# A six-operation exponential on VectorE and a shorter run-up to the first exponential, in a fused attention and feed-forward kernel

## The chip, the cores and the metric

One core of a Trainium2 chip runs the program. The metric is device time in microseconds (us), lower is better. Most executions of one kernel here lie within some 2.5 us of their median, so a difference below a few tenths of a per cent needs several rounds; the ratios below come with a 95% interval. The times go with the TensorE clock that was granted: the kernel before spanned 881.2 us in the run with a mean clock of 0.999 and 885.7 us in one with 0.993.

Engine names in the profile: PE is TensorE (PEld its weight loads), ACT is ScalarE, DVE is VectorE, POOL is GpSimd, SP issues most transfers.

## The reference

```python
def reference(A_x, A_wqkv, A_wo, B_x, B_w_gate, B_w_up, B_w_down, gate_w):   # S=2048, D=512, 32 heads of 16, F=1792
    x = A_x
    g = sigmoid((x * gate_w).sum(-1, keepdims=True))
    a = attention(x, wqkv, wo)        # softmax(q k^T / 4) v, per head, then wo
    b = (silu(x @ w_gate) * (x @ w_up)) @ w_down
    return g * a + (1 - g) * b
```

What matters is the softmax: 32 heads x 2048 queries x 2048 keys, 134 million exponentials. The kernel cuts them into 2048 score tiles of 128 keys x 512 queries.

## The kernel before

TensorE makes a score tile in PSUM. Two tiles at a time go to ScalarE, which does the exponential in one activation of 128x1024 (`e_t<-s_t`). Every so often four tiles go to VectorE instead: each is scaled and rounded to a 16-bit integer whose upper bits are those of a bf16 exponent (`y_t<-d_t`), and a polynomial in the low nine bits then corrects the mantissa over all four tiles at once.

```python
def first():        # once per tile; after the fourth tile, queue the passes over [128, 2048]
    vec.tensor_scalar(out=y[:, i*QBW:(i+1)*QBW], in0=d_t, scalar1=EXP_A, scalar2=EXP_B, op0=mult, op1=add)
    ...
    vops.extend([                    # (cost in us that the kernel's own plan charges VectorE, the pass)
        (0.73, z = y & 0x1FF),
        (0.73, u = C3*z + C2),
        (1.26, u = u * z),
        (0.73, u = (u + C1) * S),
        (1.26, u = u * z),
        (1.26, y = y + u),
        (0.73, y = y * 0.25; the block may now be multiplied with the values)])
```

That listing is abridged: each entry is a lambda around one VectorE instruction. While the program is built, a planner keeps three clocks (`plan.pe`, `plan.act`, `plan.dve`) and decides from them when VectorE is free enough to take another block. So the charged cost of a block decides how many blocks VectorE gets, and with them the order of every engine.

The run-up to the first exponential, abridged:

```python
def v_now(tt): ...                       # four matmuls of value tile tt, evacuated by ScalarE
act(out=q0r, in_=qp0, func=Copy)
for i in range(2):                       # two halves of the keys of the first heads
    vec.tensor_reduce(out=kpart0[:, i], in_=kp0[i], op=max, apply_absolute_value=True)
    vec.tensor_copy(out=ones_h[i], in_=onescol)
    v_now(i)
    act(out=kaug[...i...], in_=kp0[i], func=Identity, bias=ones_h[i])
    if i == 0: kneg1 = bsel0 * kpart0[:, 0];  aq0 = |q0r|
kneg0 = min(bsel0 * kpart0[:, 1], kneg1)
v_now(2)
mm(bp0, lhsT=kneg0, rhs=aq0)             # a bound on the scores, kept below zero in the exponent
...                                      # q0 <- q0r, then q0 += bp0
V0 = 4
v_now(3)                                 # the first exponential follows; values from V0 on are paced side work
```

Later query blocks get the same bound by `q0_pieces(qb)`: it evacuates the projection, writes |q| to `mt[:, 4:6, :]`, and a separate piece, `bound`, multiplies it. The paced side work (values, keys, queries, the feed-forward part) is placed between score tiles by deadline.

Of the kernel before, what the change touches and what calls it, by code (L numbers as in the profile page):

```python
# [9 lines left out]
ALU = mybir.AluOpType  # L10
# [68 lines left out]
def kernel(  # L79
# [12 lines left out]
    nc = tc.nc  # L92
# [4 lines left out]
    DH = 16  # L97
# [19 lines left out]



    EXP_A = 512.0 * inv_sqrt_dh * math.log2(math.e)  # L120
    EXP_B = 512.0 * 127.0

    EXP_C3, EXP_C2, EXP_C1, EXP_S = 0.0012034477878222, 1.8215637461803453, -1248.848130748923, 1.0 / 4096.0



# [32 lines left out]
    def act(*args, **kw):  # L159
        ordered(nc.scalar.activation(*args, **kw))  # L160
# [7 lines left out]
    vec = Ordered()  # L168
# [49 lines left out]
    bsel0 = mt[:, 3, 0:P]  # L218
# [3 lines left out]
    for i in range(2):  # L222
        nc.vector.tensor_copy(
            out=wpad[i][:, :, :].rearrange("p dc (j c) -> p dc j c", c=32)[:, :, :, 1:1 + DH],
# [9 lines left out]
    pidx = const.tile([P, 1], F32, name="pidx")  # L234
    nc.gpsimd.iota(pidx[:], pattern=[[0, 1]], base=0, channel_multiplier=1,
                   allow_small_or_imprecise_dtypes=True)
    bsel = const.tile([P, 8], BF16, name="bsel")
    lo_t = const.tile([P, 8], F32, name="lo_t")
    for h in range(8):
        c = 2 * (h % 4) + h // 4  # L240
        nc.gpsimd.memset(lo_t[:, c:c + 1], float(DH * h))
    far_t = const.tile([P, 8], F32, name="far_t")

    nc.vector.tensor_scalar(out=lo_t[:], in0=lo_t[:], scalar1=pidx[:, 0:1], scalar2=None, op0=ALU.subtract)
    nc.vector.tensor_scalar(out=far_t[:], in0=lo_t[:], scalar1=-float(DH) + 0.5, scalar2=-1.0,
                            op0=ALU.is_gt, op1=ALU.mult)
    nc.vector.scalar_tensor_tensor(out=bsel[:, :], in0=lo_t[:], scalar=0.5, in1=far_t[:],
                                   op0=ALU.is_lt, op1=ALU.mult)
    nc.gpsimd.memset(wo_l[:], 0.0)
    sbc_t = const.tile([P, P], BF16, name="sbc_t")  # L250
    nc.gpsimd.memset(sbc_t[:], 0.0)
# [31 lines left out]
    def spend(mode, mms, ready=0.0):  # L283

        plan.pe = max(plan.pe + (0.1 if mode != plan.mode else 0.0), ready) + (0.226 if mode == "F" else 0.216) * mms
        plan.mode = mode
# [93 lines left out]
    def v_pieces(tt, act_evac=False):  # L380
        st = {}

        def pc(h):
            def f():
                if h == 0:
                    st["p"] = m_tile("vp")
                for dc in (2 * h, 2 * h + 1):
                    mm(st["p"][:, 0:D], lhsT=xT[:, dc, tt * P:(tt + 1) * P], rhs=wv[:, dc, :],
                       start=(dc == 0), stop=(dc == DC - 1))
                spend("F", 2)  # L390
                if h == 1 and act_evac:
                    end()
                elif h == 1:
                    later(0.75, end)
            return f

        def end():
            dst = vaug[:, tt, 0:G * 4 * VC].rearrange("p (h c) -> p h c", c=VC)[:, :, 1:1 + DH]
            sv = st["p"][:, 0:D].rearrange("p (h c) -> p h c", c=DH)
            if act_evac:  # L400
                act(out=dst, in_=sv, func=ACT.Copy)
            else:
                vec.tensor_copy(out=dst, in_=sv)
            m_free(plan.pe if act_evac else plan.dve)
        return [(2, pc(0), True), (2, pc(1), False)]
# [201 lines left out]
    def score(ps, b):  # L607
        n, j = b // 4, HEADS[b % 4]
        (qb, g), kt = UNIT[n // KT], n % KT
        r = slice(64 * (j // 2), 64 * (j // 2) + 64)  # L610
        q = q0[qb][r, j % 2, :] if g == 0 else get_qx(qb, g // 2)[r, j % 2, g % 2, :]
        mm(ps, lhsT=kaug[r, g, kt * P:(kt + 1) * P], rhs=q, start=True, stop=True,
           tile_position=(64 * (j // 2), 0))
# [26 lines left out]
    def emit_d(b):  # L640
        while d_wait:
            pay_d()
        d_t = ps_d.tile([P, QBW], F32, tag="d", name="d_t")
        score(d_t[:, :], b)
        spend("R", 1, d_end[0])
        if not vcur:
            y_live[0] += 1
            blocks[b // (4 * KT)] = blocks.get(b // (4 * KT), 0) + 1
            vcur["y"] = vex.tile([P, NV * QBW], U16, tag="y", name="y_t", bufs=3)
            vcur["i"], vcur["b"] = 0, []  # L650
        y, i = vcur["y"], vcur["i"]
        vcur["i"] += 1
        vcur["b"].append(b)
        e_of[b] = y[:, i * QBW:(i + 1) * QBW].bitcast(BF16)
        block = dict(vcur)
        if i == NV - 1:
            vcur.clear()

        def first():
            vec.tensor_scalar(out=y[:, i * QBW:(i + 1) * QBW], in0=d_t[:, :], scalar1=EXP_A, scalar2=EXP_B,  # L660
                              op0=ALU.mult, op1=ALU.add)
            if i < NV - 1:
                return
            z = vex.tile([P, NV * QBW], U16, tag="z", name="z_t")
            u = vex.tile([P, NV * QBW], F16, tag="u", name="u_t")
            ya, za, ua = y[:, :], z[:, :], u[:, :]
            mine = list(block["b"])
            assert sorted(m % 4 for m in mine) == list(range(4)) and mine[0] // (4 * KT) == mine[-1] // (4 * KT)
            vops.extend([
                (0.73, lambda: vec.tensor_scalar(out=za, in0=ya, scalar1=0x1FF, scalar2=None, op0=ALU.bitwise_and)),  # L670
                (0.73, lambda: vec.tensor_scalar(out=ua, in0=za, scalar1=EXP_C3, scalar2=EXP_C2, op0=ALU.mult,
                                                 op1=ALU.add)),
                (1.26, lambda: vec.tensor_tensor(out=ua, in0=ua, in1=za, op=ALU.mult)),
                (0.73, lambda: vec.tensor_scalar(out=ua, in0=ua, scalar1=EXP_C1, scalar2=EXP_S, op0=ALU.add,
                                                 op1=ALU.mult)),
                (1.26, lambda: vec.tensor_tensor(out=ua, in0=ua, in1=za, op=ALU.mult)),
                (1.26, lambda: vec.tensor_tensor(out=ya, in0=ya, in1=ua, op=ALU.add)),
                (0.73, lambda: (vec.tensor_scalar(out=ya, in0=ya, scalar1=0.25, scalar2=None, op0=ALU.mult),
                                late.append((plan.dve + 0.4, mine)))),
            ])  # L680
        d_wait.append((plan.pe + 0.25, first))

    def pay_d():
        ready, f = d_wait.pop()
        plan.dve = max(plan.dve, ready) + 0.6
        f()
        d_end[0] = plan.dve + 0.1
# [178 lines left out]
    kpart0 = const.tile([P, 2], F32, name="kpart0")  # L866
# [4 lines left out]
    kneg1 = mt[:, 3, 2 * P:3 * P]  # L871
    def v_now(tt):
        for _, f, _ in v_pieces(tt, act_evac=True):
            f()

    act(out=q0r[:, :], in_=qp0[:, :], func=ACT.Copy)
    for i in range(2):
        vec.tensor_reduce(out=kpart0[:, i:i + 1], in_=kp0[i][:, :], axis=AX.X, op=ALU.max,
                          apply_absolute_value=True)
        vec.tensor_copy(out=ones_h[i][:], in_=onescol[:])  # L880
        v_now(i)
        act(out=kaug[:, 0, i * 2 * QBW:(i + 1) * 2 * QBW], in_=kp0[i][:, :], func=ACT.Identity,
            bias=ones_h[i][:, 0:1], scale=1.0)
        if i == 0:
            vec.tensor_scalar(out=kneg1, in0=bsel0, scalar1=kpart0[:, 0:1], scalar2=None, op0=ALU.mult)
            vec.tensor_scalar(out=aq0[:, :].bitcast(U16), in0=q0r[:, :].bitcast(U16), scalar1=0x7FFF, scalar2=None,
                              op0=ALU.bitwise_and)
    vec.scalar_tensor_tensor(out=kneg0, in0=bsel0, scalar=kpart0[:, 1:2], in1=kneg1,
                             op0=ALU.mult, op1=ALU.min)
    v_now(2)  # L890
    bp0 = ps_d.tile([P, QBW], F32, tag="d", name="bp0")
    mm(bp0[:, :], lhsT=kneg0, rhs=aq0[:, :], start=True, stop=True)
    for v in range(2):
# [1 line left out]
    for v in range(2):  # L895
        vec.scalar_tensor_tensor(out=q0[0][:, v, :], in0=bp0[:, :], scalar=vsel[:, v:v + 1],
                                 in1=q0[0][:, v, :], op0=ALU.mult, op1=ALU.add)
    V0 = 4
    v_now(3)
    plan.dve = plan.act = plan.pe  # L900


# [2 lines left out]
    v_chain = {}  # L905
    for tt in range(V0, KT):
        v_chain[tt] = pace.add(v_pieces(tt), 0, tt + 3)
# [37 lines left out]
    for qb in range(QB):  # L945
        a0 = f0 + per * qb
        for fc in range(FC):
            load, pcs = gu[(qb, fc)]
            i = order_.index((qb, fc))
# [269 lines left out]
```

## Time and profile before

| | before |
|---|---|
| median of 3 runs | 885.43 us (884.97 to 886.7) |
| span of the profiled run | 883.3 us |
| exponentials on ScalarE / blocks on VectorE | 890 / 67 |
| first exponential starts | 19.82 us |
| end of the last exponential to the end | 8.8 us |

How to read the lines: a group line gives the source line (here mostly a helper's), the engine, the operation, output<-input, shapes and count; then busy time and mean nanoseconds of one; then the engine's idle time ahead of it and what ended that idle time. The prediction below shows the lines of the kernel before.

I use one more measure. ScalarE runs the exponentials almost back to back, and its step from one start to the next has a floor of 903 ns after an exponential and 477 ns after a tanh. What a step has above its floor I call a **slip**. Slips are summed from the start times in the trace, from the first exponential to the last: 24.1 us before. (The prediction and some expectations count only slips after exponentials, above 903.5 or 905 ns; that is 0.3 to 0.8 us less.)

Not every slip need be the program's. In each of the fourteen profiles TensorE's clock stood at half in one to three stretches of about 3.4 or 6.8 us between the first exponential and the last. The view of busy time by stretch shows it, here for such a stretch before, then after (columns: stretch, its length, busy time and number of instructions of PE, PEld, DVE, ACT, POOL, then the clock, and share and GB/s of the transfers):

```profile
859.69:866.51 6.82, 5.62 (x26) 1.27 (x26) 4.08 (x8) 5.38 (x7) 0.00 (x0) 0.50 0.01 2
```

```profile
842.83:846.24 3.41, 3.17 (x23) 0.73 (x19) 3.21 (x6) 2.84 (x4) 0.00 (x0) 0.50 0.01 2
```

The slips whose step ends in such a stretch, or within 1 us of its end, come to 1.9 us before and 1.0 after, and to 1.2 to 6.0 in the other profiles. Why the clock falls is not shown here. Below, "outside half clock" means slips without these.

### The profile page before, as it was taken

The page shows a single profiled execution, that of the slowest core. Times are in us where ns is not written, and L with a number is a line of the kernel's source. Part 1 is how long each engine was busy: PE and PEld are TensorE (multiplying, and loading weights), DVE is VectorE, ACT ScalarE, POOL GpSimd, SP SyncE. Part 2 cuts the span into 40 slices and gives each one's busy share as a digit, 9 for nine tenths or more (in the row PEclk, how much of TensorE's full clock was granted, in tenths as well). Part 3 has the DMA queues.
Part 4 walks back from the last instruction along what each step waited for, and adds up shares of the span by engine and source line. Part 5 has one row for each costly group of instructions (what it writes and reads, how often), then busy time and mean ns, then how long its engine had stood idle before and what let it go on. Part 6 is the DMA issues. An engine that isn't in the chain of part 4 may idle for free.

```text
span 883.3 us, 14242 instructions
## 1 busy us (share of the span) xinstructions
PE 784.8 (89%) x5078; PEld 207.2 (23%) x5168; DVE 797.8 (90%) x1129; ACT 853.5 (97%) x955; POOL 7.0 (1%) x29
## 2 busy tenths in 40 slices
PE   6999999999998898889998888998988888989876
PEld 2222222222222222222222222222222222222211
DVE  6379999999999999998999999999999999999995
ACT  3999999999999999999999999999999999999995
POOL 3000000000000000000000000000000000000000
PEclk9999999999999999999999999999999999999998
DMA  8401021121101112110001112100011111000000
GB/s 208 108 1 33 23 50 43 34 49 28 34 7 31 34 43 64 45 34 16 5 11 35 38 42 61 48 24 10 4 32 34 36 51 44 22 11 5 4 21 24
DMA packets 87535, 31.98 MB, mean 36 GB/s; under 512 B 75120, under 2 KB 87016, under 8 KB 87464
## 3 DMA queue, kind: packets, MB, share of 16 engines
q1 hardware_dynamic: 86408, 30.94, 14.3%
q8 instruction: 40, 0.66, 0.3%
q10 hardware_dynamic: 1056, 0.13, 0.1%
q14 instruction: 31, 0.25, 0.1%
HBM read 20.83 MB, written 2.34 MB: 26 GB/s over the span
## 4 chain that ended last, share of the span: by engine, by line
ACT 40%; PE 29%; DVE 17%; issue 10%; SPq 1%; DMA 1%; DVEq 0%; ACTq 0%
ACT e_t L160 37%; PE s_t L157 11%; DVE y_t L166 7%; PE o_ps L157 6%; DVE u_t L166 5%; ACT th L160 3%; PE d_t L157 3%; PE dps L157 2%; PE gp L157 2%; PE qp L157 1%; PE up L157 1%; SPq L173 1%; DVE mt L166 1%; PE kp L157 1%; DVE gs L166 1%
## 5 line engine op out<-in xcount | busy, mean ns | idle before, releaser
L160 ACT ACTIVATE e_t<-s_t 128x1024 bf16<-128x1024 f32 x890 | 830.3, 1080 | 7.0 <-PE s_t L157 6.0
L157 PE MATMUL s_t<-qx,kaug 64*128 64x512 bf16 x1668 | 333.3, 385 | 59.9 <-ACT e_t L160 55.8
L166 DVE TENSOR_SCALAR y_t<-d_t 128x512 uint16<-128x512 f32 x268 | 184.0, 687 | 28.0 <-PE d_t L157 25.1
L157 PEld LDWEIGHTS <-kaug 64*128 64x128 bf16 x2048 | 99.3, 93 | 389.3 <-issue 387.6
L157 PE MATMUL o_ps<-e_t,vaug 128*32 128x512 bf16 x1780 | 173.1, 388 | 0.9
L166 DVE TENSOR_TENSOR u_t<-u_t,z_t 128x2048 f16<-128x2048 f16 x134 | 163.4, 1219 | 1.9
L157 PE MATMUL d_t<-qx,kaug 64*128 64x512 bf16 x252 | 95.0, 377 | 1.7 <-DVE y_t L166 1.3
L166 DVE TENSOR_TENSOR y_t<-y_t,u_t 128x2048 uint16<-128x2048 uint16 x67 | 81.6, 1218 | 0.8
L157 PEld LDWEIGHTS <-vaug 128*32 128x32 bf16 x2048 | 45.4, 94 | 136.8 <-issue 133.2
L157 PE MATMUL dps<-wd_t,mt 128*128 128x512 bf16 x200 | 62.4, 384 | 3.3 <-issue 3.3
L157 PE MATMUL gp<-xT,wg 128*128 128x512 bf16 x196 | 61.6, 384 | 2.5 <-issue 2.5
L157 PE MATMUL up<-xT,wu 128*128 128x512 bf16 x210 | 62.4, 383 | 1.5 <-issue 1.4
L166 DVE TENSOR_SCALAR y_t<-y_t 128x2048 uint16<-128x2048 uint16 x67 | 46.2, 690 | 1.3
L166 DVE TENSOR_SCALAR u_t<-z_t 128x2048 f16<-128x2048 uint16 x67 | 46.0, 686 | 0.6
L166 DVE TENSOR_SCALAR u_t<-u_t 128x2048 f16<-128x2048 f16 x67 | 45.8, 684 | 0.2
L166 DVE TENSOR_SCALAR z_t<-y_t 128x2048 uint16<-128x2048 uint16 x67 | 45.9, 685 | 0.1
L166 DVE SCALAR_TENSOR_TENSOR gs<-th,gp 128x512 bf16<-128x512 bf16 x56 | 38.2, 682 | 5.1 <-ACT th L160 4.4
L166 DVE SCALAR_TENSOR_TENSOR mt<-gs,up 128x512 bf16<-128x512 bf16 x56 | 38.2, 683 | 3.5 <-PE up L157 1.7
L160 ACT ACTIVATE th<-gp 128x512 bf16<-128x512 f32 x56 | 36.8, 657 | 0.0
L157 PEld LDWEIGHTS <-mt 128*128 128x128 bf16 x263 | 16.2, 99 | 43.8 <-issue 36.8
L157 PE MATMUL s_t<-on,kaug 64*128 64x512 bf16 x112 | 22.0, 384 | 3.3 <-ACT e_t L160 3.2
L166 DVE TENSOR_TENSOR osb<-of,x_ps 128x512 bf16<-128x512 f32 x28 | 19.1, 681 | 2.8 <-PE x_ps L157 2.7
(101 smaller groups left out, 337.8 us busy)
## 6 DMA issues: line engine op xcount, KB each, us to landing
wg<-in_B_w_gate_dram SPq DMA_DIRECT2D x56, 128.0 KB
wu<-in_B_w_up_dram SPq DMA_DIRECT2D x56, 128.0 KB
on<-osb SPq DMA_DIRECT2D x120, 16.0 KB
rb<-rr SPq DMA_DIRECT2D x15, 128.0 KB
wd_t<-in_B_w_down_dram SPq DMA_DIRECT2D x1, 1792.0 KB
qx<-qst SPq DMA_DIRECT2D x112, 16.0 KB
out_dram<-o_t SPq DMA_DIRECT2D x12, 128.0 KB
kaug<-on SPq DMA_DIRECT2D x20, 64.0 KB
```

The costliest lines, as they stand in the source:

```text
L157: ordered(nc.tensor.matmul(*args, **kw))
L160: ordered(nc.scalar.activation(*args, **kw))
L166: return lambda *a, **kw: ordered(f(*a, **kw))
L173: nc.sync.dma_start_transpose(out=xT[:, dc, :], in_=x[:, dc * P:(dc + 1) * P])
```

## The change

The intent is threefold. The cubic in z is factored, so that a pass disappears: with z' = z + 2048 (an OR), the correction is (K z' + M)^2 z' plus a constant D, which rides on the last pass. Only two value tiles are made ahead of the first exponential, and the key copies come ahead of the value evacuations on ScalarE. Three tiny constants are made after the first scores.

```diff
-    EXP_B = 512.0 * 127.0
-    EXP_C3, EXP_C2, EXP_C1, EXP_S = 0.0012034477878222, 1.8215637461803453, -1248.848130748923, 1.0 / 4096.0
+    EXP_K, EXP_M, EXP_D = 0.0005430666826427128, -1.2590564982977572, -43.5
+    EXP_B = 512.0 * 127.0 + (-44.13360029727899 - EXP_D)
 ... (vops)
-  z = y & 0x1FF;  u = C3*z + C2;  u = u*z;  u = (u + C1)*S;  u = u*z;  y = y + u;  y = y*0.25
+  z = y & 0x1FF | 0x800;  u = K*z + M;  u = u*u;  u = u*z;  y = y + u;  y = (y + D)*0.25
 ... (run-up)
         vec.tensor_copy(out=ones_h[i][:], in_=onescol[:])
-        v_now(i)
         act(out=kaug[...], in_=kp0[i][:, :], func=ACT.Identity, bias=ones_h[i][:, 0:1], scale=1.0)
         if i == 0:
-            vec.tensor_scalar(out=kneg1, in0=bsel0, scalar1=kpart0[:, 0:1], ...)
             vec.tensor_scalar(out=aq0, in0=q0r, scalar1=0x7FFF, op0=ALU.bitwise_and)
+        v_now(i)
+    vec.tensor_scalar(out=kneg1, in0=bsel0, scalar1=kpart0[:, 0:1], ...)
     vec.scalar_tensor_tensor(out=kneg0, ...)
-    v_now(2)
 ...
-    V0 = 4
-    v_now(3)
+    lo_t, far_t, bsel: three small VectorE instructions, formerly ahead of the first maximum
+    V0 = 2
```

More of the change, by code (lines that the diff above doesn't have):

```diff
@@ L242 @@
     far_t = const.tile([P, 8], F32, name="far_t")
-    nc.vector.tensor_scalar(out=lo_t[:], in0=lo_t[:], scalar1=pidx[:, 0:1], scalar2=None, op0=ALU.subtract)
-    nc.vector.tensor_scalar(out=far_t[:], in0=lo_t[:], scalar1=-float(DH) + 0.5, scalar2=-1.0,
-                            op0=ALU.is_gt, op1=ALU.mult)
-    nc.vector.scalar_tensor_tensor(out=bsel[:, :], in0=lo_t[:], scalar=0.5, in1=far_t[:],
-                                   op0=ALU.is_lt, op1=ALU.mult)
     nc.gpsimd.memset(wo_l[:], 0.0)
@@ L669, in first @@
             vops.extend([
-                (0.73, lambda: vec.tensor_scalar(out=za, in0=ya, scalar1=0x1FF, scalar2=None, op0=ALU.bitwise_and)),
-                (0.73, lambda: vec.tensor_scalar(out=ua, in0=za, scalar1=EXP_C3, scalar2=EXP_C2, op0=ALU.mult,
+                (0.73, lambda: vec.tensor_scalar(out=za, in0=ya, scalar1=0x1FF, scalar2=0x800, op0=ALU.bitwise_and,
+                                                 op1=ALU.bitwise_or)),
+                (0.73, lambda: vec.tensor_scalar(out=ua, in0=za, scalar1=EXP_K, scalar2=EXP_M, op0=ALU.mult,
                                                  op1=ALU.add)),
-                (1.26, lambda: vec.tensor_tensor(out=ua, in0=ua, in1=za, op=ALU.mult)),
-                (0.73, lambda: vec.tensor_scalar(out=ua, in0=ua, scalar1=EXP_C1, scalar2=EXP_S, op0=ALU.add,
-                                                 op1=ALU.mult)),
+                (1.26, lambda: vec.tensor_tensor(out=ua, in0=ua, in1=ua, op=ALU.mult)),
                 (1.26, lambda: vec.tensor_tensor(out=ua, in0=ua, in1=za, op=ALU.mult)),
                 (1.26, lambda: vec.tensor_tensor(out=ya, in0=ya, in1=ua, op=ALU.add)),
-                (0.73, lambda: (vec.tensor_scalar(out=ya, in0=ya, scalar1=0.25, scalar2=None, op0=ALU.mult),
+                (0.73, lambda: (vec.tensor_scalar(out=ya, in0=ya, scalar1=EXP_D, scalar2=0.25, op0=ALU.add,
+                                                  op1=ALU.mult),
                                 late.append((plan.dve + 0.4, mine)))),
@@ L884 @@
         if i == 0:
-            vec.tensor_scalar(out=kneg1, in0=bsel0, scalar1=kpart0[:, 0:1], scalar2=None, op0=ALU.mult)
             vec.tensor_scalar(out=aq0[:, :].bitcast(U16), in0=q0r[:, :].bitcast(U16), scalar1=0x7FFF, scalar2=None,
                               op0=ALU.bitwise_and)
+        v_now(i)
+    vec.tensor_scalar(out=kneg1, in0=bsel0, scalar1=kpart0[:, 0:1], scalar2=None, op0=ALU.mult)
     vec.scalar_tensor_tensor(out=kneg0, in0=bsel0, scalar=kpart0[:, 1:2], in1=kneg1,
                              op0=ALU.mult, op1=ALU.min)
-    v_now(2)
     bp0 = ps_d.tile([P, QBW], F32, tag="d", name="bp0")
@@ L897 @@
                                  in1=q0[0][:, v, :], op0=ALU.mult, op1=ALU.add)
-    V0 = 4
-    v_now(3)
+    vec.tensor_scalar(out=lo_t[:], in0=lo_t[:], scalar1=pidx[:, 0:1], scalar2=None, op0=ALU.subtract)
+    vec.tensor_scalar(out=far_t[:], in0=lo_t[:], scalar1=-float(DH) + 0.5, scalar2=-1.0,
+                            op0=ALU.is_gt, op1=ALU.mult)
+    vec.scalar_tensor_tensor(out=bsel[:, :], in0=lo_t[:], scalar=0.5, in1=far_t[:],
+                                   op0=ALU.is_lt, op1=ALU.mult)
+    V0 = 2
     plan.dve = plan.act = plan.pe
```

## The prediction

> **What bounds the kernel now.** I read the page from the top: first the busy line, then the chain that ended last, then the costliest groups.
>
> ```profile
> PE 784.8 (89%) x5078; PEld 207.2 (23%) x5168; DVE 797.8 (90%) x1129; ACT 853.5 (97%) x955; POOL 7.0 (1%) x29
> ...
> ACT 40%; PE 29%; DVE 17%; issue 10%; SPq 1%; DMA 1%; DVEq 0%; ACTq 0%
> ...
> L160 ACT ACTIVATE e_t<-s_t 128x1024 bf16<-128x1024 f32 x890 | 830.3, 1080 | 7.0 <-PE s_t L157 6.0
> ...
> L166 DVE TENSOR_SCALAR y_t<-d_t 128x512 uint16<-128x512 f32 x268 | 184.0, 687 | 28.0 <-PE d_t L157 25.1
> L166 DVE TENSOR_TENSOR u_t<-u_t,z_t 128x2048 f16<-128x2048 f16 x134 | 163.4, 1219 | 1.9
> L166 DVE TENSOR_TENSOR y_t<-y_t,u_t 128x2048 uint16<-128x2048 uint16 x67 | 81.6, 1218 | 0.8
> L166 DVE TENSOR_SCALAR y_t<-y_t 128x2048 uint16<-128x2048 uint16 x67 | 46.2, 690 | 1.3
> L166 DVE TENSOR_SCALAR u_t<-z_t 128x2048 f16<-128x2048 uint16 x67 | 46.0, 686 | 0.6
> L166 DVE TENSOR_SCALAR u_t<-u_t 128x2048 f16<-128x2048 f16 x67 | 45.8, 684 | 0.2
> L166 DVE TENSOR_SCALAR z_t<-y_t 128x2048 uint16<-128x2048 uint16 x67 | 45.9, 685 | 0.1
> ```
>
> The reader is to see three things. ScalarE (ACT) is busy 97% of an 883.3 us span, and the 890 exponentials of 128x1024 were held up for only 7.0 us that the groups show as idle. VectorE (DVE) and TensorE (PE) are each near 90%, so neither has much to spare. And 2048 score tiles of 128x512 are shared between two engines: 890 x 2 = 1780 go to ScalarE, 268 = 67 blocks of four go to VectorE, which spends the last seven operations on each block. The chain gives ScalarE only 40%, because it hops at each step between three nearly full engines; I trust the busy line here.
>
> ScalarE's cost of one exponential is not the 1080 ns of the group, since neighbours overlap. From the start times in the trace, 577 of the 890 start-to-start steps are below 910 ns, and their floor is 903 ns. A tanh takes 477 ns of ScalarE in the same measure. So the ScalarE line adds up: first exponential at 19.82, 890 x 0.9035 = 804.1, 56 x 0.477 = 26.7, about 23.3 of steps longer than the floor (TensorE late by 0.1 to 1.2 us some 60 times, and many slips of 20 ns), about 0.5 for the gate's tanh, and 8.7 from the end of the last exponential to the end of the program: 883.1 against a span of 883.3.
>
> Ahead of the first exponential ScalarE is not full, so I took the order of time of the first 20 us (start, duration, engine, what):
>
> ```profile
> 13.47 1.23 DVE L166 TENSOR_REDUCE kpart<-kp 128x1 f32<-128x1024 f32 x1 [0.99 <-PE kp L157]
> ...
> 15.19 1.22 DVE L166 TENSOR_REDUCE kpart<-kp 128x1 f32<-128x1024 f32 x1
> 15.91 0.60 ACT L160 ACTIVATE vaug<-vp 128x512 bf16<-128x512 f32 x1 [1.19 <-PE vp L157]
> ...
> 16.44 0.35 DVE L166 SCALAR_TENSOR_TENSOR mt<-mt,kpart 128x128 bf16<-128x128 bf16 x1
> ...
> 17.44 0.38 PE L157 MATMUL bp<-aq,mt 128*128 128x512 bf16 x1
> ...
> 17.85 1.41 DVE L166 SCALAR_TENSOR_TENSOR qx<-bp,vsel,qx 128x512 bf16<-128x512 f32 x2 [0.53 <-PE bp L157]
> ...
> 18.05 1.02 PE L157 MATMUL vp<-rb,xT 128*128 128x512 bf16 x4 [0.23 <-ACT vaug L160]
> ...
> 18.87 1.10 ACT L160 ACTIVATE vaug<-vp 128x512 bf16<-128x512 f32 x2
> 19.00 0.70 PE L157 MATMUL s_t<-qx,kaug 64*128 64x512 bf16 x4
> ```
>
> The bound's matmul (bp) had its operand at 16.44 + 0.35 = 16.79 but ran at 17.44, behind twelve value matmuls. The first pair of score matmuls needs only the first half of qx (ready about 17.85 + 0.70 = 18.55), yet ran at 19.00, behind the fourth value tile, and the exponential came at 19.82 behind that tile's evacuation on ScalarE. The two extra value tiles are what the start waits for.
>
> **What the Trainium skill says.** "VectorE: DVE Perf Modes", section "The perf-mode tier table", gives for 2048 bf16 elements in SBUF 693 ns for tensor_scalar and 1224 ns for tensor_tensor, and says that single-source operations reach twice the rate. The trace agrees: 684 to 690 and 1218 to 1219 ns, for uint16 and f16 as well. "DVE: scalar operands, raw-bit mode, write accounting and state across instructions", section "Raw-bit mode", has AND and OR exact on a zero-extended uint16 stream, so a fused AND, OR should be one pass; no row here shows the fused pair yet. "ScalarE: Activation LUTs", section "What ACT_TABLE_LOAD costs", has an activation with immediate scale and bias at 186 + 0.833 N ns with neighbours overlapping by about 93 ns: 186 + 853 - 93 = 946 ns for N = 1024. The trace has 903, and I use 903. "Perfetto Trace Analysis", section "Identifying the Most-Contended Engine", has the engine with the highest occupancy as the one to optimize first, and warns that TensorE's matmul busy share says little; that fits the choice of ScalarE.
>
> **The change, part by part.**
>
> (a) *One VectorE pass less per block.* The removed pass is the tensor_scalar u_t<-u_t of 684 ns. The square u*u is a tensor_tensor in place of u*z (both 1219, assuming that reading one tile twice costs as reading two); the OR and the final add ride as second operations in passes that exist. A block goes from 4 x 0.687 + 4 x 0.686 + 3 x 1.219 = 9.15 us (four evacuations of d_t, four passes, three products or sums) to 8.46 us. On VectorE by itself this is worth nothing to the end, as VectorE is not the bound.
>
> (b) *What it frees is turned into more blocks.* The kernel hands out tiles as it is built, so I built the changed kernel and counted its order of instructions, which holds no times. It has 71 blocks in place of 67: 882 exponentials of 128x1024, 284 evacuations of d_t. TensorE's matmuls are the same in number and shape. ScalarE therefore loses 8 x 0.9035 = **7.2 us**, all of it on the bounding line. VectorE's exponentials go from 67 x 9.15 = 613 to 71 x 8.46 = 601 us; two more value evacuations at 0.69 bring VectorE to about 797.8 - 12 + 1.4 = 787 us, still about 90% of a shorter span.
>
> (c) *The start.* Two value tiles (eight matmuls, two 0.5 us evacuations on ScalarE) leave. In the new order ScalarE takes the first key copy ahead of the first value evacuation, and TensorE has eight value matmuls, the bound, then the scores. My timing: first maximum 13.47 to 14.70 as now; the 128x1 copy and |q| (0.28) follow; second maximum at about 15.0 instead of 15.19; kneg is no earlier, as both its steps (0.25 and 0.35) now follow the second maximum: ready about 16.8. The value matmuls end about 16.7 (14.85 + 8 x 0.22), so bp runs near 16.95 to 17.35, the first half of qx is done by 18.1, scores run 18.15 to 18.55, and the first exponential starts near 18.7 rather than 19.82: **1.1 us**. ScalarE is free by then (last evacuation about 17.9). So both maxima in a row gain almost nothing, and the missing value tiles nearly all.
>
> (d) *The small constants* (0.11 + 0.16 + 0.16 us on VectorE) move behind qx, where VectorE idles 1.45 us. Worth under 0.1 us.
>
> (e) *Given back.* 1.75 us of value matmuls now fall among the first exponentials, where TensorE is fullest (18.64 us of matmul records in the stretch from 20 to 40). TensorE's total wait for ScalarE is 59.0 us in the view of waits; the same matmuls must fit in 8 us less, so the 23.3 us of slips may grow. I choose +0.9 us, a twenty-fifth of the slips.
>
> Sum: -7.2 - 1.1 + 0.9 = -7.4, from 885.43 to **878.0 us** (0.8% faster).
>
> **The rivals.** *TensorE becomes the bound.* For it: 89% busy, slips of ScalarE that all end on s_t, and more blocks mean more lone d_t and x_ps work. Against it: 59 us of waits for ScalarE, spread over 158 places. If half the saving were lost, the time would be about 881.5. *VectorE runs late.* The kernel's order assumes 0.73 and 1.26 us for passes (measured 0.69 and 1.22) but 0.6 for evacuations (0.69). A block of the new kind is 0.09 us dearer than assumed, of the old kind 0.05, so TensorE may meet y_t not yet written; those waits (o_ps and x_ps on y_t or gs) are 7.5 us now. Doubled, they would put the time at 882 to 885. *The fused passes fall out of the fast mode*: a tensor_scalar at the 1.2 us rate would add some 0.5 us x 71 per pass, 36 us on VectorE, and make it the bound, 890 or more. The existing two-operation passes at 684 ns speak against it. *Better than the sum*: VectorE has lower load and the slips shrink by 3 us, giving 874.
>
> **Range and chances.** The 7.2 is a count by a measured floor and nearly sure; the start is sure to some 0.4 us; the slips are the doubt, from -3 to +4 us. That makes 874.0 to 882.0 for eight in ten. Two per cent is 17.7 us, over twice all that I can add up: 0.02 for faster. Slower by two per cent needs a fallen perf mode: 0.02.
>
> **What would show it right or wrong.** In the changed profile: 882 e_t activations with the floor at 903 ns; three tensor_scalar passes and three tensor_tensor passes of 71 each at 0.69 and 1.22 us, no fourth; VectorE near 787 us; first exponential at 18.5 to 19.0; tail after the last exponential 8.7 us as now; ScalarE's slips near 24 us. It is wrong if e_t's idle goes well above 10 us with PE s_t as its releaser, if a fused pass takes over 0.8 us, or if the first exponential does not move.

## The result

The changed kernel took **878.49 us** (median of 4 runs, 877.44 to 881.16); the kernel before, with a run beside it, 885.59. The ratio is 0.9923, interval 0.9899 to 0.9947. Ratios in this document divide the mean time of one kernel's runs by that of the other's of the same rounds, so they are not quite the ratio of the quoted medians. Outputs were correct in all kernels shown here. In numbers the prediction of 878.0 was met. The experiments show that two of its terms were wrong and cancelled.

The page of the changed kernel, the busy line and the groups that answer to those shown of before:

```profile
PE 783.2 (89%) x5076; PEld 206.5 (24%) x5168; DVE 789.5 (90%) x1104; ACT 845.4 (97%) x945; POOL 7.0 (1%) x29
...
L161 ACT ACTIVATE e_t<-s_t 128x1024 bf16<-128x1024 f32 x882 | 823.4, 1084 | 7.6 <-PE s_t L158 5.8
...
L167 DVE TENSOR_SCALAR y_t<-d_t 128x512 uint16<-128x512 f32 x284 | 195.1, 687 | 29.1 <-PE d_t L158 25.4
...
L167 DVE TENSOR_TENSOR u_t<-u_t 128x2048 f16<-128x2048 f16 x71 | 86.6, 1220 | 1.0
L167 DVE TENSOR_TENSOR y_t<-y_t,u_t 128x2048 uint16<-128x2048 uint16 x71 | 86.6, 1219 | 1.0
L167 DVE TENSOR_TENSOR u_t<-u_t,z_t 128x2048 f16<-128x2048 f16 x71 | 86.3, 1215 | 0.3
...
L167 DVE TENSOR_SCALAR y_t<-y_t 128x2048 uint16<-128x2048 uint16 x71 | 48.8, 688 | 1.0
L167 DVE TENSOR_SCALAR u_t<-z_t 128x2048 f16<-128x2048 uint16 x71 | 48.8, 687 | 0.8
L167 DVE TENSOR_SCALAR z_t<-y_t 128x2048 uint16<-128x2048 uint16 x71 | 48.6, 684 | 0.1
```

The count of exponentials went from 890 to 882, and the removed pass is gone: six passes of 71. The fused AND, OR takes 684 ns, as the AND alone took 685; the square of one tile takes 1220 ns, as the product of two took 1219. ScalarE is as full as before (97%), VectorE too (90%): what the pass freed was spent on more blocks.

The two profiled runs add up as follows.

| us | before | after | difference |
|---|---|---|---|
| start of the first exponential | 19.8 | 19.6 | -0.2 |
| exponentials at the 903 ns floor | 803.7 (890) | 796.4 (882) | -7.2 |
| slips ahead of 150 us | 3.1 | 6.8 | +3.7 |
| slips after 150 us | 21.0 | 17.0 | -4.0 |
| last exponential's end to the end | 8.8 | 8.8 | 0.0 |
| sum of differences (56 tanh unchanged) | | | -7.7 |
| span | 883.3 | 875.7 | -7.6 |

Of the later slips, 1.9 us before and 1.0 after are those at half clock, so the fall outside half clock is from 19.1 to 16.0: 3.1 us, not 4.0. The tail of 8.8 us is not fixed either: in four of the later profiles, with the clock at half during it, it was 9.8 to 10.3 us.

The third row is new, and no stretch at half clock lies in it. It also shows in the view of busy time by stretch, without any sum of mine: the row from 20 to 150 us of each kernel, first before, then after (columns: stretch, its length, then busy time and number of instructions for PE, PEld, DVE, ACT, POOL, then clock and transfers).

```profile
20.00:150.00 130.00, 121.48 (x805) 33.49 (x817) 105.33 (x152) 129.42 (x145) 0.00 (x0) 1.00 0.18 44
```

```profile
20.00:150.00 130.00, 119.37 (x787) 32.53 (x801) 103.48 (x150) 126.06 (x140) 0.00 (x0) 1.00 0.18 42
```

ScalarE is busy 129.42 of 130 us before and 126.06 after, with five instructions fewer done by then. Something in the changed kernel leaves ScalarE waiting early on.

The start, in order of time, of the changed kernel:

```profile
6.09 1.97 DVE L224 COPY mt<-wqk 128x256 bf16<-128x256 bf16 x1 [1.76 <-DMA wqk<-in_A_wqkv_dram]
6.13 1.81 POOL L405 MEMSET qx<- 128x2048 bf16 x1
...
14.58 1.23 DVE L167 TENSOR_REDUCE kpart<-kp 128x1 f32<-128x1024 f32 x1 [1.82 <-PE kp L158]
...
15.71 1.89 PE L158 MATMUL vp<-rb,xT 128*128 128x512 bf16 x8 [0.52 <-DMA rb<-in_A_wqkv_dram]
...
15.90 1.11 ACT L161 ACTIVATE kaug<-kp,ones_h 128x1024 bf16<-128x1024 f32 x1
...
17.95 0.39 PE L158 MATMUL bp<-aq,mt 128*128 128x512 bf16 x1 [0.36 <-DVE mt L167]
...
19.18 0.39 PE L158 MATMUL s_t<-qx,kaug 64*128 64x512 bf16 x2 [0.84 <-DVE qx L167]
19.61 5.12 ACT L161 ACTIVATE e_t<-s_t 128x1024 bf16<-128x1024 f32 x5 [0.62 <-PE s_t L158]
```

From the first maximum to the first exponential it is now 19.61 - 14.58 = 5.03 us, against 19.82 - 13.47 = 6.35 before: 1.3 us shorter. But this run's first maximum was 1.1 us later. The first two lines show why: the weights landed a little late, the copy that pads them met the GpSimd fill of another buffer, and a copy of 0.26 us took 1.97.

### The profile page after: what moved, and what is told of

It is laid out like the page before. It is cut to its first block, busy times and chain, and to the rows that moved or that the text cites. A ratio compares the mean times of both kernels' runs of the same rounds, so it can differ in the third digit from the quotient of the medians. Undisturbed runs are those within 1.5% of the kernel's fastest.

```text
span 875.7 us, 14203 instructions
## 1 busy us (share of the span) xinstructions
PE 783.2 (89%) x5076; PEld 206.5 (24%) x5168; DVE 789.5 (90%) x1104; ACT 845.4 (97%) x945; POOL 7.0 (1%) x29
## 4 chain that ended last, share of the span: by engine, by line
ACT 40%; PE 38%; DVE 10%; issue 10%; DMA 1%; ACTq 0%; DVEq 0%; SPq 0%
ACT e_t L161 37%; PE s_t L158 14%; PE o_ps L158 7%; DVE y_t L167 4%; PE d_t L158 4%; PE dps L158 3%; ACT th L161 3%; PE gp L158 2%; DVE u_t L167 2%; PE up L158 2%; PE kp L158 2%; PE qp L158 1%; PE vp L158 1%; PE a_ps L158 1%; DVE mt L167 1%
## 5 line engine op out<-in xcount | busy, mean ns | idle before, releaser
L167 DVE TENSOR_SCALAR y_t<-d_t 128x512 uint16<-128x512 f32 x284 | 195.1, 687 | 29.1 <-PE d_t L158 25.4
L158 PE MATMUL d_t<-qx,kaug 64*128 64x512 bf16 x264 | 99.7, 377 | 0.3
L167 DVE TENSOR_TENSOR u_t<-u_t 128x2048 f16<-128x2048 f16 x71 | 86.6, 1220 | 1.0
L167 DVE TENSOR_TENSOR y_t<-y_t,u_t 128x2048 uint16<-128x2048 uint16 x71 | 86.6, 1219 | 1.0
L167 DVE TENSOR_TENSOR u_t<-u_t,z_t 128x2048 f16<-128x2048 f16 x71 | 86.3, 1215 | 0.3
L167 DVE TENSOR_SCALAR y_t<-y_t 128x2048 uint16<-128x2048 uint16 x71 | 48.8, 688 | 1.0
L167 DVE TENSOR_SCALAR u_t<-z_t 128x2048 f16<-128x2048 uint16 x71 | 48.8, 687 | 0.8
L167 DVE TENSOR_SCALAR z_t<-y_t 128x2048 uint16<-128x2048 uint16 x71 | 48.6, 684 | 0.1
L167 DVE CAST vaug<-vp 128x512 bf16<-128x512 f32 x14 | 9.7, 691 | 15.5 <-PE vp L158 15.5
```

The costliest lines, as they stand in the source:

```text
L158: ordered(nc.tensor.matmul(*args, **kw))
L167: return lambda *a, **kw: ordered(f(*a, **kw))
```

## The experiments

The theories. **A**: the number of exponentials on ScalarE sets the time; VectorE's relief pays only through it. **B**: VectorE's relief itself pays. **C**: slips eat a part of what the exponentials give. **D**: the shorter start pays what it saves. Against D, after the first results, **E**, **F** and **J**: the two deferred value tiles take the gain back early on, by one misplaced bound (E), by projections that land among VectorE's exponentials (J), or by crowding in general (F). **G**: the collision with GpSimd costs time. **H**: VectorE has no more room. Twelve kernels ran, each with five rounds beside the kernel before. Whatever follows from one profile each is said so.

### One pass fewer, the same hand-out

The plan still charges seven passes; one entry issues nothing. TensorE's and ScalarE's orders are identical to those of before.

```diff
-  u = C3*z + C2;  u = u*z;  u = (u + C1)*S  (0.73);  u = u*z; ...
+  u = K*z + M;    u = u*u;  nothing         (0.73);  u = u*z; ...      # and the new constants
```

> The six-operation exponential in the kernel before, while the hand-out of tiles still charges VectorE for the seventh pass (an entry that issues nothing). TensorE's and ScalarE's orders are then the same as before, 890 exponentials, 67 blocks; VectorE just has 67 x 0.684 = 46 us less. Theory A (ScalarE's count of exponentials sets the time): 885 us, at most 1.5 us better, by fewer waits of TensorE for a late y_t. Rival B (VectorE's relief itself shortens the run): 4 us or more off, 881 or lower.

Measured: 885.43 us against 885.38, ratio 0.9993 (0.9978 to 1.0009). The busy line and two groups of this kernel:

```profile
PE 786.6 (89%) x5078; PEld 206.8 (23%) x5168; DVE 757.8 (86%) x1062; ACT 853.5 (96%) x955; POOL 7.1 (1%) x29
...
L159 ACT ACTIVATE e_t<-s_t 128x1024 bf16<-128x1024 f32 x890 | 830.1, 1078 | 7.0 <-PE s_t L156 6.2
...
L165 DVE TENSOR_SCALAR y_t<-d_t 128x512 uint16<-128x512 f32 x268 | 184.2, 687 | 51.0 <-PE d_t L156 48.8
```

VectorE lost 40 us of busy time (797.8 to 757.8), and its idle time before y_t<-d_t rose from 28.0 to 51.0 us. I had expected 46: the 684 ns of the group overlap with the neighbours, and a removed pass frees 40 / 67 = 0.60 us. The time did not move, so B, which asked for 4 us or more, falls. The slips stayed at 24.0, but 3.2 of them are at half clock against 1.9 before; outside half clock the later slips are 17.5 us against 19.1. A small gain, as A allowed it (at most 1.5 us), is not excluded by the interval.

### The exponential alone, with its hand-out

```diff
 kernel before, with the six passes and constants of the change; the run-up untouched
```

> The six-operation exponential with its new hand-out, the start as before. The built order has 71 blocks and 882 exponentials. Theory A: 8 x 0.9035 = 7.2 us off, 878.4 us within 1.5, first exponential where it was, slips of ScalarE near 23 us. Rival B: no more than what pass_only gives. Rival C (slips eat part of it): 880 to 882.

Measured: 875.75 us, ratio 0.9895 (0.9878 to 0.9913): about 9.3 us off, more than the 7.2 that 8 exponentials give. The ratio is below the full change's 0.9923, though the intervals overlap. In its profile the slips are 21.2 us, 2.9 less than before: 3.3 ahead of 150 us, 17.8 after. So A holds with an addition: this kernel also slips less later on. Outside half clock the later slips are 19.1 us before, 17.5 in pass_only and 16.3 here, so relief and new order may each have a part; from one profile each, this is not shown. Rival C falls.

### The new start alone

```diff
 the changed kernel, with the seven passes and constants of before
```

> The new start with the seven-operation exponential. The first exponential should come 1.1 to 1.3 us sooner after the first maximum (6.35 us before). But the two value evacuations that move to VectorE cost it a block: the built order has 66 blocks and 892 exponentials, 2 x 0.9035 = 1.8 us more on ScalarE. Theory A: these cancel, 886.1 us within 1.5. Rival D (the start's gain is the whole of it, as my prediction has it): 884.3.

Measured: 886.83 us, ratio 1.0024 (1.0009 to 1.0039): 2.1 us **slower** than before. The first exponential is 5.03 us after the first maximum, as said, and there are 892 exponentials, 1.8 us more, which is most of the loss. Its early slips are 5.0 us against 3.1. D, which asked for 884.3, falls: the new start alone does not pay what it saves.

### Two value tiles fewer, alone

```diff
-    v_now(2)
 ...
-    V0 = 4
-    v_now(3)
+    V0 = 2
```

> Only the two value tiles fewer ahead of the first exponential; the order of the maxima and the small constants as before. It has the same orders on TensorE from there on as start_only, 66 blocks, 892 exponentials. If the missing value tiles are nearly all of the start's gain, as my working has it: within 0.4 us of start_only, and the first exponential 5.0 to 5.4 us after the first maximum. If the maxima in a row matter: 1 us slower than start_only and the first exponential 6 us after the first maximum.

Measured: 888.06 us, ratio 1.0031 (1.0014 to 1.0048), not told apart from start_only. The first exponential came 5.69 us after the first maximum, between the two forecasts. Here it waited for the second key copy on ScalarE, which stood behind two value evacuations; putting the key copies first is what the reordering adds.

### Where the start's gain went: one misplaced bound?

In the changed kernel the built order has |q| of block 3 written to the one buffer shared by the blocks (`mt[:, 4:6, :]`) ahead of the bound of block 2. The order of time around 64 us:

```profile
62.94 0.43 DVE L167 TENSOR_SCALAR mt<-on 128x1024 uint16<-128x1024 uint16 x1
...
65.43 0.43 DVE L167 TENSOR_SCALAR mt<-on 128x1024 uint16<-128x1024 uint16 x1
65.91 0.59 PE L158 MATMUL bp<-mt 128*128 128x512 bf16 x2 [1.70 <-DVE mt L167]
...
66.92 1.94 ACT L161 ACTIVATE e_t<-s_t 128x1024 bf16<-128x1024 f32 x2 [1.53 <-PE s_t L158]
```

The bound of block 2, whose own |q| was written by 62.94 + 0.43 = 63.37, waits 1.70 us for the second write, and ScalarE idles 1.53. The block gets another block's bound. Softmax does not change when a row is shifted, and the output passed its comparison, but it is a fault of ordering that the kernel before did not show.

```diff
-        q = pace.add(q, 0, d - 6)
+        q = pace.add(q, 0, d - 6, prev)      # wait until the previous block's bound is emitted
         bd = pace.add(bd, 0, d - 4, [q])
+        prev = [bd]
```

> The changed kernel, with the query projection of a block held back until the bound of the block before it is emitted. In the changed kernel the |q| of block 3 is written to the one buffer that holds the |q| of block 2 before TensorE has read it, so the bound of block 2 waits 1.70 us for VectorE at 64 us and is taken from the wrong block (softmax does not mind). Theory E (this is where the start's gain went): that slip is gone, ScalarE's slips fall from 23.6 to about 21.5, and the ratio to before is 0.990 to 0.991 rather than the changed kernel's 0.9923. Rival F (the two extra value tiles crowd TensorE in general): 0.992 to 0.993 and slips near 23.6, only elsewhere.

Measured: 877.64 us, ratio 0.9900 (0.9885 to 0.9916). The ratio is what E forecast, the slips are not: 25.8 us, 7.4 of them ahead of 150. That slip is gone, and another of 2.05 us stands at 71 us, where a score tile for VectorE waits 1.95 us behind the evacuation of the same projection:

```profile
73.03 0.58 PE L158 MATMUL d_t<-qx,kaug 64*128 64x512 bf16 x1 [1.95 <-DVE y_t L167]
```

```profile
72.70:76.20 3.50, 3.17 (x19) 0.73 (x18) 3.39 (x5) 1.94 (x2) 0.00 (x0) 0.51 0.02 5
```

The second line shows that the clock was at half just there. 2.8 of the 7.4 us end in that stretch or within 1 us of it; the wait of 1.95 us had begun before it, so only a part of them is the clock's, and this profile alone does not refute E. The times speak against it: qx_dve (below), which keeps the misplaced bound, has a mean of 877.87 us against 877.88 here, at mean clocks of 0.995 and 0.994, and after_four is 2.1 us faster by the medians. E as the whole cause falls; the fault is mended.

### The change with four value tiles

```diff
     vec.scalar_tensor_tensor(out=kneg0, ...)
+    v_now(2)
 ...
-    V0 = 2
+    V0 = 4
+    v_now(3)
```

> The changed kernel with four value tiles ahead of the first exponential instead of two; all else, the order of maxima, key copies and constants, as changed. 71 blocks, 882 exponentials, bounds in their right order. Theory E and F both: slips near 21 as in exp_only. The start: first exponential 5.9 to 6.4 us after the first maximum, against 5.03 with two tiles and 6.35 to 6.50 in the kernel before. Ratio to before 0.989 to 0.990, as exp_only (0.9895). If the order of maxima costs something itself: 0.992.

Measured: 875.52 us, ratio 0.9878 (0.9863 to 0.9893). Against 0.9925 (0.9906 to 0.9943) for the changed kernel repeated below, the intervals do not touch: the two deferred tiles cost about 4 us, estimated from these two ratios (0.0047 x 885), or 2.1 to 2.4 against the medians of the two-tile kernels (bound_order and qx_dve), whose runs are all slower than its slowest. The second figure is the safer one: the runs of after_again had a mean clock of 0.993, those of after_four 0.995. They were run at other times. In the profile the slips are 21.9 us (4.5 early) against 23.9 (6.8 early), and 1.1 of the 4.5 are at half clock; the first exponential is 6.02 us after the first maximum. So with two tiles 1.0 us of start is won and 6.8 - 3.4 = 3.4 of early slips are lost, a loss of 2.4.

### The fill of the query buffer moved off GpSimd

```diff
-    nc.gpsimd.memset(qx[0][:], 0.0)
 ... (after the small constants)
+    vec.memset(qx[0][:].bitcast(F32), 0.0)
```

> The changed kernel with the zeroing of the first query buffer moved from GpSimd (1.81 us from 6.1) to VectorE's idle time after the start. In the changed kernel's profile a weight copy of VectorE that normally takes 0.26 us took 1.97 us beside that GpSimd fill, and the first matmul came at 8.11 instead of about 6.1. Theory G (the two collide whenever the weights land late): first matmul at 5.9 to 6.5 us here, and times up to 1 us shorter than the changed kernel's and less scattered. Rival (the late weights alone set it): no difference beyond noise.

Measured: 877.95 us (876.67 to 878.78), ratio 0.9905 (0.9891 to 0.9920). The first matmul is at 5.75 us and the first exponential at 18.38, but the collision did not happen in the repeated run of the changed kernel below either (first matmul 5.64). It depends on when the weights land. The gain in time is not told apart from noise; G stays open.

### The new hand-out with seven passes

```diff
 six-pass hand-out; the entry for u*z issues two instructions, (u + C1)*S and u*z, and is charged for one
```

> The changed kernel's hand-out and its TensorE and ScalarE orders (882 exponentials, 71 blocks), but with the seven-operation exponential: VectorE has 71 x 0.684 = 48.6 us more, some 838 us. Theory A strictly (the count of exponentials on ScalarE alone sets the time): 878.5. Theory H (VectorE must have the room that the removed pass gives, or TensorE waits for y_t): ScalarE's slips rise by 4 us or more and the time is 883 to 890. I expect H, 885.

Measured: 896.93 us, ratio 1.0117 (1.0097 to 1.0138), slower than before and than I expected. The group of exponentials and one line of its view of waits (who waited for whom: total us, times, longest), then the same line of the changed kernel:

```profile
L162 ACT ACTIVATE e_t<-s_t 128x1024 bf16<-128x1024 f32 x882 | 826.8, 1069 | 24.3 <-PE s_t L159 21.3
```

```profile
PE o_ps L159 <- DVE y_t L168: 11.4, 19, 1.2
```

```profile
PE o_ps L158 <- DVE y_t L167: 1.0, 4, 0.3
```

With the same 882 exponentials the slips are 45.0 us, and TensorE waits 11.4 us for a late y_t where it waited 1.0 us in the changed kernel. VectorE is busy 828.6 us, 39 more. 6.0 of the 45.0 are at half clock, against 1.0 of 23.9, which does not change the picture. So in this hand-out the 71 blocks need the pass gone. That VectorE could not carry them at all is not shown: it is busy for 92% of this longer span, and the plan did not know of the seventh pass. A strictly taken falls, H holds.

### The changed kernel again

```diff
 no change
```

> The changed kernel once more, as the control on this chip and for its first matmul: 878.5 us within 1, ratio 0.991 to 0.9925, ScalarE's slips 23.6 in all and about 6.8 us of them before 150 us, with one of 1.70 us at about 64.

Measured: 878.31 us, ratio 0.9925 (0.9906 to 0.9943). The slips are 24.4 us, 6.8 of them early, and again one of 1.69 us at 63.6. The early slips belong to the program, not to one run. Here the first exponential is at 18.90 us, 5.83 after the first maximum but 3.38 after the first value matmul at 15.52, which waits for the value weights to land. Five of the profiles with the full new start have 3.37 or 3.38 us between these two. In the other three the first maximum was less than 1.5 us ahead of the weights, and the first exponential came 5.03 to 5.06 us after the maximum. With four tiles and the new order it is 4.76 (after_four, cheap_four), with the old start 4.97 to 4.98 (before, exp_only); pass_only has 5.97, with the clock at half from 15.66 to 19.07 us, where its value matmuls ran. So the later of two things starts the exponentials, and the landing of the value weights is one of them.

### The projections of later query blocks earlier

```diff
-        q = pace.add(q, 0, d - 6)
-        bd = pace.add(bd, 0, d - 4, [q])
+        q = pace.add(q, 0, d - (6 if qb == 1 else 16), prev)
+        bd = pace.add(bd, 0, d - (4 if qb == 1 else 14), [q])
+        prev = [bd]
```

> The changed kernel (two value tiles) with the deadlines of the query projections of blocks 2 and 3 moved ten slots earlier, and each held until the bound before it is emitted. As built, both then fall between VectorE's first blocks of exponentials, as with four tiles, in place of into the second of them. Theory J (the two deferred tiles push these projections, whose evacuation takes VectorE 1.84 us, into a block of exponentials, where d_t and the bound wait for VectorE): slips before 150 us fall from 6.8 to 3.5 to 4.7, all slips to about 21, the start's gain stays (5.03 us), ratio 0.987 to 0.989, about 2 us below after_again. Rival F (two tiles crowd TensorE wherever): slips stay above 6 before 150 us and the time within 1 us of after_again.

Measured: 877.29 us, ratio 0.9907 (0.9890 to 0.9924), not told apart from after_again. Early slips fall only to 5.7 us: a bound still waits 1.6 us for VectorE, now the one of block 3, right behind its projection. The later slips are 19.6 us against the 17.5 of after_again, but 2.9 and 1.2 of them are at half clock, which leaves 16.7 and 16.3. J is neither shown nor excluded; it explains a part of the early slips at most.

### Both together

```diff
 q_earlier and qx_dve in one
```

> q_earlier with the zeroing of the first query buffer on VectorE, to combine what helped: 0 to 1 us below q_earlier, first matmul at 5.7 to 6.5 us. The best so far is after_four at 0.9878; if theories G and J both hold, this is 0.986 to 0.988.

Measured: 875.74 us, ratio 0.9902 (0.9886 to 0.9918). A miss: no better than after_four.

### More blocks for VectorE

```diff
-  passes charged at 0.73 and 1.26 us      (after_four)
+  passes charged at 0.69 and 1.20 us
```

> after_four with VectorE's passes charged at 0.69 and 1.20 us (measured 0.69 and 1.22) instead of 0.73 and 1.26, so that it takes on 73 blocks and ScalarE has 878 exponentials. Theory A: 4 x 0.9035 = 3.6 us less than after_four (0.9878), 0.984. Theory H (VectorE has no more room: seven_new's 39 us more of busy VectorE cost 21 us of slips): two blocks are 17 us more on VectorE, slips up by 4 to 9 us, 0.989 to 0.994. I expect H, near 0.990.

Measured: 873.33 us, ratio 0.9871 (0.9854 to 0.9889), the fastest here. Against after_four's 0.9878 it is not told apart. There are 878 exponentials, 3.6 us less. The slips rose from 21.9 to 24.2 us, but 4.8 of these are at half clock against 2.2 in after_four; outside half clock they are 19.4 and 19.7. So the profile does not show that the two blocks cost slips. The interval excludes both forecasts, 0.984 of A and 0.989 or more of H; how much room VectorE has left stays open.

## Why the prediction was right or wrong

- **The bound and its cost**: right. The floor stayed at 903 to 904 ns in every kernel, and the count of exponentials was worth its 7.2 us.
- **(a) A pass by itself is worth nothing**: right, 0.9993 in pass_only. The working took a pass for 684 ns and a block for 9.15 us, the sum of mean durations, which overlap; a pass frees 0.60 us (pass_only). For ScalarE it had used the steps.
- **(b) The freed time turned into blocks**: right in count (71, 882) and in VectorE's busy time (789.5, forecast 787). seven_new adds what I had only argued: in this hand-out the blocks need the pass gone.
- **(c) The start, 1.1 us**: the length was right, 1.3 us in like terms, but it is not what reached the end. (In the profile of the result the first exponential is at 19.61 us, not at the forecast 18.5 to 19.0, as the weights landed late; in after_again it is at 18.90.) "Two fewer value tiles" is a net loss: in exp_only and after_four, which keep four tiles, the ratios are 0.9895 and 0.9878 against 0.9923 and 0.9925. The step that failed took a shorter start as time off the end; the runs show 1.0 us of start won and 3.4 us of early slips lost with two tiles (after_four). Also wrong was "both maxima in a row gain almost nothing, and the missing value tiles nearly all": the tiles alone took 0.66 us off the 6.35 from maximum to exponential, tiles and reordering together 1.32 (and the reordering with four tiles 0.33). What the reordering gains is the key copies ahead of the value evacuations on ScalarE, which I had noted and not counted.
- **(d) The small constants**: not tested by itself.
- **(e) Slips, +0.9**: the term that was mis-sized in both directions. Early slips grew by 3.7 us, later ones fell by 4.0. The first belongs to the two tiles (3.3 early in exp_only, 6.8 with two tiles; with two tiles and the old hand-out 4.9 to 5.0), the second in part to the clock (0.9 of the 4.0 us), the rest to relief and the new hand-out (outside half clock 19.1 before, 17.5 in pass_only, 16.3 in exp_only). I had put down one small number where two larger ones stood.
- So the sum -7.2 - 1.1 + 0.9 met the total, while the runs give about -9.3 for the exponential and +2 to +2.7 for the start (2.1 to 2.4, 2.5 to 2.7 from exp_only's ratio to the changed kernel's). That the total was met to 0.5 us is luck.
- **The rivals**: the fused passes did not lose their speed. TensorE did not become the bound. VectorE being late is real, and seven_new shows its size when overdone.

What stays open: which of the displaced pieces makes the early slips. One bound at 64 us accounts for 1.7 of the 3.7, but mending it or moving it produced other slips of like size. Also open is how the later fall in slips divides between relief and order, and how much of it is the luck of an order; each hand-out here has one order only.

## What to carry to other kernels

When two engines share one kind of work by a plan, a pass saved on the helper pays only if the plan hands it more work: test the pass with the hand-out frozen, and the hand-out without the pass, before crediting either. Work moved out of the run-up is not gone, so look at the first hundred microseconds after it for what it displaces. A total that agrees with the forecast is no proof of its terms. And before a wait in one profile is explained, look at the clock granted in that stretch.

## What the Trainium skill lacked or had wrong

- "ScalarE: Activation LUTs", section "What ACT_TABLE_LOAD costs": its 186 + 0.833 N ns, less 93 for overlap, gives 946 ns a step for 1024 columns and 519 for 512; the runs show 903 and 477, both 42 to 43 less. The section does not say where its operands lie. "Perfetto Trace Analysis", section "Optimizing Scalar/DVE Operations", puts the access overhead of ScalarE at about 93 ns on SBUF and 51 on PSUM, and these inputs are in PSUM: those 42 ns are the difference, if the first figure is for SBUF; no run here tests it.
- "DVE: scalar operands, raw-bit mode, write accounting and state across instructions", section "Raw-bit mode", gives no time for two fused bit operations on uint16. Measured: 684 ns for AND, OR over 2048 columns, against 685 for AND alone.
- No page that I read says whether a tensor_tensor that reads one tile twice differs from one that reads two. Measured: 1220 ns against 1219.
- "SBUF — State Buffer", section "Who interferes with whom", has GpSimd and the two-port modes of VectorE exclude each other for a whole instruction. The trace agrees that the two exclude each other: the copy of 0.26 us took 1.97 beside a GpSimd fill of 1.81, in the one of two profiles of the same kernel in which a landing put the two together. The same copy earlier on took 1.26 us in tiles_only and 1.15 in after_four, beside a fill of 0.95. The trace does not show the page's rule that the one that starts first wins: the copy's record starts at 6.09 us, ahead of the fill's at 6.13, and ends after it, at 8.06 against 7.94. Spans on GpSimd are rough, so this decides nothing.
